# An attention and SoLU kernel: PE planned as two servers, the rows' factor on DVE, more row scaling on POOL

## The chip, the core and the metric

The kernel runs on one core of a Trainium2 chip. The core has five engines, each with its own in-order queue: PE (TensorE, matmuls), ACT (ScalarE), DVE (VectorE), POOL (GpSimd) and SP (SyncE, which here starts every DMA). They wait for each other through semaphores. The metric is the device time of one execution in microseconds (us): the median of three runs is 1230.0 (1227.59 to 1230.04).

## The reference

Four sets of N = 12608 rows of C = 128 numbers go through two attentions with m = 32 inducing points, and every row then through a SoLU layer: 1024 hidden values, a softmax gate, a layer norm and a projection back to 128.

```
def mab(q, kv):
    s = scale * (q @ kv.transpose(0, 2, 1))
    s = s - s.max(-1, keepdims=True)
    a = np.exp(s)
    a /= a.sum(-1, keepdims=True) + 1e-09
    return a @ kv
h = mab(I, x)                       # 32 rows for each set
x = mab(x, h)                       # 4 * 12608 rows
...
h = x @ w_in
e = np.exp(h - np.max(h, axis=-1, keepdims=True))
solu = h * e / (np.sum(e, axis=-1, keepdims=True) + 1e-09)
mu = np.mean(solu, axis=-1, keepdims=True)
var = np.mean((solu - mu) ** 2, axis=-1, keepdims=True)
ln = (solu - mu) / np.sqrt(var + 1e-06) * g_ln
return ln @ w_out
```

## The kernel before

The rows of a set are cut into 99 tiles of 128 rows, 396 tiles in all. Four tiles make a group (25 for each set), three groups a finish (9 for each set, 36 in all).

A set first runs through phase 1, `p1` (the attention of the inducing points: transposes L552, scores L660, sums L742), twelve tiles at a time, then `p2` (the rows' attention weights: scores L857, transposes L552). For the first set, phase 1 fills the first 50 us or so; for the others it is slipped in among the tiles of the set before. Then each tile goes through these steps:

- PE, L959: the tile's h (128 x 1024), in four quarters. The factor of w_in and the attention's result is held as 32 rows in each of PE's four groups of 32 rows; even tiles use the groups 0 and 1 ("pair 0"), odd ones the groups 2 and 3 ("pair 1").
- DVE, L997: negated and normalised h into an `hn` buffer, with its smallest value. These buffers lie partly in a tensor that the profile calls `spare`.
- ACT, L1007: the exponential, with its sum, into an `eu` buffer (or `spare`).
- POOL, L1011: h times the exponential, in place.
- ACT, L1022: the square, for its sum alone. DVE, L1035: a transpose of 32 x 32 blocks into `vt`.
- After four tiles, PE, L1081: the products with w_out, 32 steps of K = 32 for each of the four row groups; a column of ones (129 columns) gives the row sums. The groups 0 and 1 add up in `op_661`, 2 and 3 in `op_662`; each has a single buffer, in which three groups lie side by side.
- After twelve tiles, `evacuate` (L1106) copies `op` to `spare`, on DVE or on ACT, and `finish` turns the sums into one factor for each row: two ACT squares (L1133, L1134), three POOL instructions (L1137 to L1139: the variance), ACT's logarithm and exponential (L1144, L1145: the inverse root), four POOL instructions (L1150 to L1153: a Newton step). All of them are 12 columns wide, one for each quarter of a tile. Then each group's rows are scaled, by four ACT instructions (L1168) or by one of POOL (L1164), and stored.

The order on every engine is written out when the program is built. A planner (`Planner.run`) holds a clock for each engine, costs in ns for each item (`Op`), and priorities (lower goes first). It repeatedly takes the engine that can start soonest, and from the items ready there within `SLACK` the one of the best priority. Where an item has an `alt`, two engines compete for it. PE is one such engine: a "beat" of 225 ns is one step of both pairs, and `beats` puts the products of the other pair beside a tile's quarters (`mm1`) or transposes (`turned_rows`); `driver` emits the products that are left, for both pairs at once. What `beats` pairs is decided once, when the item starts.

Of the kernel before, what the change touches and what calls it, by code (L numbers as in the profile page):

```python
# [13 lines left out]
AF = mybir.ActivationFunctionType  # L14
# [62 lines left out]
WOUT = -11.5
WIN = -18.5
# [47 lines left out]
class Planner:  # L126


    def __init__(self, slack):
# [56 lines left out]

    def _pe(self, start, cost):

        at = start
        while True:  # L190
# [8 lines left out]
            self.busy[k] = self.busy.get(k, 0.0) + took  # L199
            at += took  # L200
            cost -= took / rate
# [3 lines left out]
    def _fill(self, until):  # L205

        for lock in self.scratch:
            if lock.free:
                buf, after = lock.free[0]
                at = max([self.clock["PE"]] + [d.end + AFTER[d.eng]["PE"] for d in after if d is not None])  # L210
# [4 lines left out]
                if at > begun:  # L215
                    self.clock["PE"] = at
# [3 lines left out]
    def run(self):  # L220
        clock = self.clock
        while self.ops:
            first = min(self.ops, key=lambda o: (max(clock[o[0].eng], o[1]), o[3]))
            eng = first[0].eng
            limit = max(clock[eng], first[1]) + self.slack[eng]
            pick = min(
                (o for o in self.ops if o[0].eng == eng and o[1] <= limit),
# [4 lines left out]
            start = max(clock[eng], ready)  # L232
            if eng == "PE" and start - clock[eng] > FILL:
# [3 lines left out]
            end = start + (self._pe(start, op.cost) if eng == "PE" else op.cost)  # L237
            clock[eng] = end
# [1049 lines left out]
```

## Time and profile before

| | |
|---|---|
| median of three runs | 1230.0 us |
| the profiled execution's own time | 1227.1 us |
| its span, first to last instruction | 1225.3 us |
| mean granted TensorE clock | 0.981 |
| DMA, mean rate over the span | 93 GB/s |

A row of the stretches has the stretch in us, its length, then for each engine its busy time and, in brackets, the number of instructions; then the granted clock, and the DMA engines' share and rate. A row of the groups has the line, engine, operation, the tile written and those read, shapes and count; then busy time in us and the mean of one in ns; then how long the engine was idle just before, and on whom it waited. The busy time counts overlapping instructions once. A row of the timeline has its start, its length, and what ran, with the number of merged instructions.

### The profile page before, as it was taken

To read this page: it belongs to the slowest core of one execution; us is meant where nothing else is said; L and a number is where in the kernel's file an instruction comes from. 1 tells how busy PE (TensorE), PEld (TensorE's weight loads), DVE (VectorE), ACT (ScalarE), POOL (GpSimd) and SP (SyncE) were. 2 spreads that over 40 slices of the span, in tenths; PEclk is the share of its full clock that TensorE was granted. 3 is DMA by queue.
4 is the path that set the end of the run, shared out by engine and by line. 5 is a ranking of instruction groups with operands and counts; after the bars stand their busy time and mean duration, and the time that the engine had idled before them with its cause. 6 is when DMAs were issued, how large, how long until landed. Compare 5 with 4: busy or idle time off the path is not lost.

```text
span 1225.3 us, 79047 instructions
## 1 busy us (share of the span) xinstructions
PE 1180.9 (96%) x35679; PEld 1091.4 (89%) x35679; DVE 1114.9 (91%) x1745; ACT 1151.3 (94%) x2479; POOL 1051.5 (86%) x758
## 2 busy tenths in 40 slices
PE   8889999999999999999999999999999999999996
PEld 6678988999899988998999999999888999998986
DVE  5669999999989999999999999999999999999992
ACT  5459999999999999999999999999999999999995
POOL 2568988889888989889889989988898999999994
PEclk9869999999999999999999999999999999999989
DMA  9462443321222324333223144433222121211111
GB/s 362 160 163 74 116 133 116 116 88 35 82 82 87 108 86 131 89 109 102 71 82 100 45 124 128 123 111 90 64 56 82 36 58 55 56 48 45 32 30 35
DMA packets 134866, 113.69 MB, mean 93 GB/s; under 512 B 79072, under 2 KB 87168, under 8 KB 134400
## 3 DMA queue, kind: packets, MB, share of 16 engines
q1 hardware_dynamic: 134528, 108.63, 29.8%
q8 instruction: 279, 4.57, 1.5%
q14 instruction: 59, 0.48, 0.1%
HBM read 54.30 MB, written 52.18 MB: 87 GB/s over the span
## 4 chain that ended last, share of the span: by engine, by line
PE 56%; ACT 21%; DVE 8%; issue 7%; POOL 4%; DMA 2%; SPq 1%; POOLq 0%; ACTq 0%; DVEq 0%
PE op L1081 36%; PE h L959 11%; ACT sq L1022 9%; ACT eu L1007 5%; DVE spare L997 3%; ACT os L1168 2%; POOL eu L1011 2%; DVE vt L1035 2%; PE h L552 2%; ACT spare L1007 1%; PE h L742 1%; PE h L660 1%; PE h L857 1%; DVE spare L1106 1%; DVE hn L997 1%
## 5 line engine op out<-in xcount | busy, mean ns | idle before, releaser
L1081 PE MATMUL op<-wc,vt 32*128 32x129 f32 x25600 | 1000.4, 275 | 11.4 <-ACT spare L1106 4.3
L1081 PEld LDWEIGHTS op<-wc,vt 32*128 32x128 f32 x25600 | 958.2, 186 | 49.3 <-issue 33.0
L1011 POOL TENSOR_TENSOR eu<-spare,eu 128x1024 f32<-128x1024 f32 x192 | 453.3, 2374 | 44.1 <-ACT eu L1007 40.7
L959 PE MATMUL h<-hs,aT 32*128 32x128 f32 x6336 | 438.0, 279 | 10.7 <-DVE spare L997 5.7
L959 PEld LDWEIGHTS h<-hs,aT 32*128 32x128 f32 x6336 | 393.7, 191 | 31.2 <-DVE spare L997 9.6
L1035 DVE STREAM_TRANSPOSE vt<-eu 128x1024 f32<-128x1024 f32 x330 | 401.1, 1228 | 7.2 <-POOL eu L1011 7.1
L1011 POOL TENSOR_TENSOR eu<-hn,eu 128x1024 f32<-128x1024 f32 x138 | 326.3, 2377 | 35.0 <-ACT eu L1007 32.2
L1022 ACT ACTIVATE sq<-eu 128x1024 bf16<-128x1024 f32 x330 | 345.9, 1048 | 6.4 <-POOL eu L1011 3.8
L997 DVE TENSOR_SCALAR_CACHE_REDUCE spare<-h,rn 128x1024 f32<-128x1024 f32 x228 | 286.3, 1263 | 23.5 <-PE h L959 12.6
L997 DVE TENSOR_SCALAR_CACHE_REDUCE hn<-h,rn 128x1024 f32<-128x1024 f32 x168 | 211.3, 1263 | 15.9 <-PE h L959 5.8
L1007 ACT ACTIVATE eu<-spare,nm 128x1024 f32<-128x1024 f32 x192 | 218.8, 1140 | 3.7 <-DVE spare L997 3.6
L1007 ACT ACTIVATE eu<-hn,nm 128x1024 f32<-128x1024 f32 x138 | 157.2, 1139 | 0.0
L1168 ACT ACTIVATE os<-spare,fin 128x128 f32<-128x128 f32 x356 | 110.5, 389 | 2.2 <-POOL fin L1153 1.2
L1011 POOL TENSOR_TENSOR spare<-spare 128x1024 f32<-128x1024 f32 x36 | 85.5, 2374 | 4.1 <-ACT spare L1007 4.1
L1035 DVE STREAM_TRANSPOSE vt<-spare 128x1024 f32<-128x1024 f32 x66 | 81.2, 1231 | 0.0
L1011 POOL TENSOR_TENSOR spare<-hn,spare 128x1024 f32<-128x1024 f32 x30 | 71.2, 2374 | 11.0 <-ACT spare L1007 8.1
L1022 ACT ACTIVATE sq<-spare 128x1024 bf16<-128x1024 f32 x66 | 69.2, 1049 | 2.5 <-POOL spare L1011 1.6
L1022 ACT ACTIVATION_READ_ACCUMULATOR sq<-eu 128x1 f32 x330 | 62.9, 190 | 0.0
L1106 DVE COPY spare<-op 128x774 f32<-128x774 f32 (+1 forms) x40 | 34.6, 865 | 15.1 <-PE op L1081 9.5
L552 PE MATMUL h<-ident,xn 32*128 32x32 f32 x1188 | 46.0, 220 | 0.9 <-issue 0.6
L552 PEld LDWEIGHTS h<-ident,xn 32*128 32x128 f32 x1188 | 44.6, 137 | 2.1 <-issue 1.0
L1007 ACT ACTIVATE spare<-spare,nm 128x1024 f32<-128x1024 f32 x36 | 41.1, 1141 | 0.0
(164 smaller groups left out, 967.8 us busy)
## 6 DMA issues: line engine op xcount, KB each, us to landing
xT<-xd SPq DMA_DIRECT2D x96, 256.0 KB, 3.2
out_dram<-os SPq DMA_DIRECT2D x96, 256.0 KB, 2.5
xn<-in_x_dram SPq DMA_DIRECT2D x73, 256.0 KB, 3.1
xd<-xT SPq DMA_DIRECT2D x72, 256.0 KB, 2.6
dl<-dd SPq DMA_DIRECT2D x396, 1.0 KB, 2.7
xd<-vt SPq DMA_DIRECT2D x7, 768.0 KB, 10.1
spare<-in_x_dram SPq DMA_DIRECT2D x5, 768.0 KB, 12.5
wc<-hn SPq DMA_DIRECT2D x16, 128.0 KB, 3.0
```

Source lines behind the costliest of these rows:

```text
L552: nc.tensor.transpose(out=tr[:h, at : at + M], in_=block[rows, :h], identity=ident[rows, rows])
L660: nc.tensor.matmul(sc[g * M : (g + 1) * M, : nn * M], lhsT=indT, rhs=xT[:, :nn, g * M : (g + 1) * M], start=True, stop=True)
L742: nc.tensor.matmul(pooled[q * M : (q + 1) * M, :], lhsT=ew[:, s, :], rhs=xn[:, s, :], start=(s < 4), stop=(s + 4 >= n))
L959: nc.tensor.matmul(hp[:, cols], lhsT=aT[rows, i // 2, :], rhs=hs[rows, cols], start=True, stop=True)
L997: lambda: nc.vector.tensor_scalar(out=hn, in0=hp, scalar1=rn, scalar2=None, op0=ALU.mult, op1=ALU.min, accum_out=nm),
L1007: "ACT", 1133, lambda: nc.scalar.activation(e, hn, AF.Exp, bias=nm, scale=-1.0, accum_out=G["qe"][:, s, 1:2]), d, rel, srel,
L1011: d = yield Op("POOL", 2330, lambda: nc.gpsimd.tensor_tensor(out=e, in0=hn, in1=e, op=ALU.mult), de, prio=t + PR_MU)
L1022: "ACT", 1040, lambda: nc.scalar.activation(sq, e, AF.Square, scale=1.0 / 32.0, accum_out=G["qe"][:, s, 0:1]), d,
L1035: lambda: nc.vector.transpose(out=G["vtb"][:, : n * FF].rearrange("p (j s t) -> p j s t", j=M, s=n)[:, :, s, :], in_=e.rearrange("p (a f) ...
L1081: nc.tensor.matmul(op[:rows, a - 2 * w, i * (C + 1) : (i + 1) * (C + 1)], lhsT=vt[q, k, :], rhs=wc[q, k, :], start=(k == 0), stop=(k == JB ...
L1106: return lambda: eng(F["raw"][:rows, : 4 * k, :].rearrange("p (j a) c -> p j a c", a=4)[:, :, 2 * w : 2 * w + 2].rearrange("p j a c -> p a ...
L1168: nc.scalar.activation(os[:rows, q, :], raw[:, q, :], AF.Copy, scale=y[:, i0 + q : i0 + q + 1])
```

## The change

**PE as two servers.** The planner gets a clock for each pair, `PE0` and `PE1`; an item of "PE" needs both. Each quarter of a tile's h is now an item of its own pair, so are each three transposes, and each pair has its own `driver`; `beats` and `closing` are gone. **The factor.** ACT's square L1134 goes; three DVE instructions make the variance and three the Newton step, in place of the seven of POOL. **Scaling and evacuation** get priorities by engine, and POOL's cost goes from 1000 to 1040. Most of the tuning numbers change, among them `HN_MORE` (one of the shared buffers goes from `hn` to `eu`) and `FIRST` (the first attention group has six tiles, not four).

```
-JC = 1
-BEAT = 225
-EAGER = 120
+BEAT = 224
-HN_MORE = 4
+HN_MORE = 3
-FIRST = 4
+FIRST = 6
+PR_SA = 13.21
+PR_SP = 41.78
+PR_ED = 17.72
+PR_EA = -19.55
+TURN_NS = 62
+SMALL = 125
+PARTS = {"PE": ("PE0", "PE1")}
-SLACK = {"PE": 0, "ACT": 100, "DVE": 300, "POOL": 0, "SP": 0}
+SLACK = {"PE": 28, "ACT": 52, "DVE": 252, "POOL": 154, "SP": 0}
...
+    def free(self, eng):
+        return max(self.clock[e] for e in PARTS.get(eng, (eng,)))
...
-            first = min(self.ops, key=lambda o: (max(clock[o[0].eng], o[1]), o[3]))
+            first = min(self.ops, key=lambda o: (max(self.free(o[0].eng), o[1]), o[3]))
...
+            same = {eng, "PE"} if eng in PARTS["PE"] else {eng, *PARTS.get(eng, ())}
             pick = min(
-                (o for o in self.ops if o[0].eng == eng and o[1] <= limit),
+                (o for o in self.ops if o[0].eng in same and o[1] <= limit),
...
-            clock[eng] = end
+            for e in PARTS.get(eng, (eng,)):
+                clock[e] = end
...
-        count = -(-len(blocks) // TURNS)
-        return Op("PE", count * BEAT, lambda: beats(count, (1 - w,), some), *after, prio=prio)
+        d = after
+        for i in range(0, len(blocks), TURNS):
+            d = yield Op(f"PE{w}", TURN_NS * min(TURNS, len(blocks) - i) + 10, some(i), d, prio=prio)
+        return d
...
-            d = yield Op("PE", 4 * BEAT, mm1, aT_d, hw_d, rel, prio=t - 50)
-            closing(d)
+            d = yield Op(f"PE{i % 2}", BEAT, quarter(0), aT_d, hw_d, rel, prio=t - 50)
+            for c in range(1, 4):
+                d = yield Op(f"PE{i % 2}", BEAT, quarter(c), d, prio=t - 60)
...
             def step():
-                op.cost = BEAT * beats(JC)
+                p["emit"](2 * w, p["j"])
+                p["emit"](2 * w + 1, p["j"])
+                p["j"] += 1
+
+            d = yield Op(f"PE{w}", BEAT, step, Done("PE", p["ready"]), prio=p["prio"])
...
-            "DVE", 90 + 269 * k, copied(nc.vector.tensor_copy), dop, rel, prio=prio,
-            alt=Op("ACT", 90 + 215 * k, copied(nc.scalar.copy), dop, rel, prio=prio),
+            "DVE", 90 + 269 * k, copied(nc.vector.tensor_copy), dop, rel, prio=prio + PR_ED,
+            alt=Op("ACT", 90 + 215 * k, copied(nc.scalar.copy), dop, rel, prio=prio + PR_EA),
...
-        d = yield Op("ACT", 110, lambda: nc.scalar.activation(part, F["raw"][:rows, :w, C], AF.Square, scale=1.0 / FF), F["out"])
         def variance():
-            gt(out=v, in0=Q, in1=part, op=ALU.subtract)
-            gs(out=v, in0=v, scalar1=0.0, scalar2=None, op0=ALU.max)
-            gt(out=v, in0=v, in1=ep, op=ALU.add)
-        d = yield Op("POOL", 760, variance, fd, d)
+            sums = F["raw"][:rows, :w, C]
+            stt(out=part, in0=sums, scalar=-1.0 / FF**2, in1=sums, op0=ALU.mult, op1=ALU.mult)
+            tt(out=v, in0=part, in1=Q, op=ALU.add)
+            stt(out=v, in0=v, scalar=0.0, in1=ep, op0=ALU.max, op1=ALU.add)
+        d = yield Op("DVE", 3 * SMALL, variance, fd, F["out"])
...
         def newton():
-            gt(out=z, in0=root, in1=root, op=ALU.mult)
-            gt(out=z, in0=z, in1=v, op=ALU.mult)
-            gs(out=z, in0=z, scalar1=-0.5, scalar2=1.5, op0=ALU.mult, op1=ALU.add)
-            gt(out=y, in0=z, in1=root, op=ALU.mult)
-        dy = yield Op("POOL", 1010, newton, d)
+            tt(out=z, in0=root, in1=root, op=ALU.mult)
+            stt(out=z, in0=z, scalar=-0.5, in1=v, op0=ALU.mult, op1=ALU.mult)
+            stt(out=y, in0=z, scalar=1.5, in1=root, op0=ALU.add, op1=ALU.mult)
+        dy = yield Op("DVE", 3 * SMALL, newton, d)
...
-            done = yield Op("ACT", 1170, scaled_act, dy, rel, alt=Op("POOL", 1000, scaled, dy, rel))
+            done = yield Op("ACT", 1170, scaled_act, dy, rel, prio=prio + PR_SA, alt=Op("POOL", 1040, scaled, dy, rel, prio=prio + PR_SP))
```

In the program that comes out, row scalings stand on ACT for 41 groups in place of 89 (164 instructions in place of 356) and on POOL for 59 in place of 11; evacuations on ACT 70 times in place of 32 and on DVE 2 in place of 40. The lines of the new program are a few lower: L1004 is the former L1011, L951 the former L959, L1074 the former L1081, L990 the former L997, L1028 the former L1035, and `op_633`, `op_634` are the former `op_661`, `op_662`.

**POOL and DVE at the thirteenth finish**, in the second set. POOL's queue before, with multiplies around the factor:

```order
L1137 TENSOR_TENSOR fin_111<-dl_110,fin_111 128x12
L1138 TENSOR_SCALAR fin_111<-fin_111 128x12
L1139 TENSOR_TENSOR fin_111<-fin_111 128x12
L1011 TENSOR_TENSOR spare<-spare 128x1024
L1150 TENSOR_TENSOR fin_111<-fin_111 128x12
L1151 TENSOR_TENSOR fin_111<-fin_111 128x12
L1152 TENSOR_SCALAR fin_111<-fin_111 128x12
L1153 TENSOR_TENSOR fin_111<-fin_111 128x12
```

DVE's queue after, at the same finish (`hn_81` is a tile's L990, `small_123` belongs to phase 1 of the next set):

```order
L1130 SCALAR_TENSOR_TENSOR fin_113<-spare 128x12
L1131 TENSOR_TENSOR fin_113<-fin_113,dl_112 128x12
L1132 SCALAR_TENSOR_TENSOR fin_113<-fin_113 128x12
L990 TENSOR_SCALAR hn_81,nm_117<-h_631,rn_97 128x1024
L688 TENSOR_SCALAR small_123,m_126<-h_632,m_126 128x4
L695 TENSOR_SCALAR small_123<-m_126 128x1
L1143 TENSOR_TENSOR fin_113<-fin_113 128x12
L1144 SCALAR_TENSOR_TENSOR fin_113<-fin_113 128x12
L1145 SCALAR_TENSOR_TENSOR fin_113<-fin_113 128x12
L1028 STREAM_TRANSPOSE vt<-spare 128x32x32
```

The seven have left POOL's queue; DVE has two threes instead, with one tile's L990 and two small instructions between them, and transposes behind.

**ACT and POOL where rows are scaled.** ACT's queue before, after the same finish:

```order
L1144 ACTIVATE fin_111<-fin_111 128x12
L1145 ACTIVATE fin_111<-fin_111 128x12
L1007 ACTIVATE eu,qe_108<-spare,nm_115 128x1024
L609 COPY xT<-h_660 128x12x64
L1168 ACTIVATE os_100<-spare,fin_111 128x128 x4
L1168 ACTIVATE os_101<-spare,fin_111 128x128 x4
L1022 ACTIVATE sq,qe_108<-eu 128x1024
```

POOL's queue after, in the second set (L1156 is the former L1164):

```order
L1004 TENSOR_TENSOR spare<-spare 128x1024
L1156 TENSOR_TENSOR os_101<-spare,fin_113 128x512
L1004 TENSOR_TENSOR spare<-spare 128x1024
L1156 TENSOR_TENSOR os_100<-spare,fin_113 128x512
L1004 TENSOR_TENSOR eu<-hn_81,eu 128x1024
```

Where ACT had eight scalings in a row ahead of a tile's square, POOL now has one instruction for each group, between two multiplies.

**PE where the first products start.** Before (`h_659` and `h_660` are tiles' h, each row of `x2` one step of a pair):

```order
L959 MATMUL h_659<-hs_119,aT_96 128x128 x8
L1081 MATMUL op_661<-wc,vt 128x129 x2
L1081 MATMUL op_662<-wc,vt 128x129 x2
L1081 MATMUL op_661<-wc,vt 128x129 x2
L1081 MATMUL op_662<-wc,vt 128x129 x2
```

After:

```order
L951 MATMUL h_631<-hs_119,aT_96 128x128 x8
L951 MATMUL h_632<-hs_119,aT_96 128x128 x4
L1074 MATMUL op_633<-wc,vt 128x129 x2
L951 MATMUL h_632<-hs_119,aT_96 128x128 x2
L1074 MATMUL op_633<-wc,vt 128x129 x4
L951 MATMUL h_632<-hs_119,aT_96 128x128 x2
L1074 MATMUL op_633<-wc,vt 128x129 x2
L1074 MATMUL op_634<-wc,vt 128x129 x2
```

Before, a tile's four quarters were one item, and the products began after it; now products of the other pair stand between the quarters of a tile that is already under way.

More of the change, by code (lines that the diff above doesn't have):

```diff
@@ L88, with kind @@
 DMA_GAP = 25
-BEGIN = {"PE": 1290.0, "ACT": 1700.0, "DVE": 2100.0, "POOL": 1300.0, "SP": 550.0}
+BEGIN = {"PE0": 1290.0, "PE1": 1290.0, "ACT": 1700.0, "DVE": 2100.0, "POOL": 1300.0, "SP": 550.0}
 DMA_RATE = 360.0
 WINDOW = 4096 / 1.2
+def kind(eng):
+    return "PE" if eng[:2] == "PE" else eng
 class Done:
@@ L198, in _pe @@
             took = min(room, cost * rate)
[L199 removed]
+            self.busy[k] = self.busy.get(k, 0.0) + max(0.0, at + took - max(at, self.until))
             at += took
+            self.until = max(self.until, at)
             cost -= took / rate
@@ L209, in _fill @@
                 buf, after = lock.free[0]
-                at = max([self.clock["PE"]] + [d.end + AFTER[d.eng]["PE"] for d in after if d is not None])
+                at = max([self.free("PE")] + [d.end + AFTER[kind(d.eng)]["PE"] for d in after if d is not None])
                 begun = at
@@ L231, in run @@
             op, ready, task = pick[:3]
-            start = max(clock[eng], ready)
-            if eng == "PE" and start - clock[eng] > FILL:
+            eng = op.eng
+            start = max(self.free(eng), ready)
+            if kind(eng) == "PE" and start - self.free("PE") > FILL:
                 self._fill(start - SPARE)
@@ L236, in run @@
             op.fn()
-            end = start + (self._pe(start, op.cost) if eng == "PE" else op.cost)
-            clock[eng] = end
+            end = start + (self._pe(start, op.cost) if kind(eng) == "PE" else op.cost)
+            for e in PARTS.get(eng, (eng,)):
+                clock[e] = end
             if eng == "SP":
@@ L1090, in close @@
             give(TURN[w], None)
-        ready = max(d.end + AFTER[d.eng]["PE"] for a in (G["turned"], rel, wc_ready.after) for d in a if d is not None)
+        ready = max(d.end + AFTER[kind(d.eng)]["PE"] for a in (G["turned"], rel, wc_ready.after) for d in a if d is not None)
         stream[w].update(j=0, emit=emit, ready=ready, close=close, prio=t + PR_G2)
-        idle = flow["idle"]
+        idle = flow[w]["idle"]
         if idle.waiting:
@@ L1259, in set_attention_then_solu_kernel @@
     spawn(main(), 0)
-    spawn(driver(), 0)
+    for w in range(2):
+        spawn(driver(w), 0)
     plan.run()
```

119 lines of the change are left out of this document (48 added, 71 removed).

## The prediction

> **What bounds the kernel now.** I read the page first, then the busy time by stretches (0 to 80 us, where the first batch is read; 80 to 1200 us, where all four engines work on tiles; the end).
>
> ```profile
> span 1225.3 us, 79047 instructions
> ...
> PE 1180.9 (96%) x35679; PEld 1091.4 (89%) x35679; DVE 1114.9 (91%) x1745; ACT 1151.3 (94%) x2479; POOL 1051.5 (86%) x758
> ...
> PE 56%; ACT 21%; DVE 8%; issue 7%; POOL 4%; DMA 2%; SPq 1%; POOLq 0%; ACTq 0%; DVEq 0%
> ```
>
> ```profile
> core 0: us, PE busy (x) PEld busy (x) DVE busy (x) ACT busy (x) POOL busy (x), PEclk, DMA share, GB/s
> 0.00:80.00 80.00, 66.36 (x703) 51.09 (x705) 48.80 (x135) 42.53 (x97) 32.13 (x34) 0.87 0.67 229
> 80.00:1200.00 1120.00, 1098.77 (x34490) 1025.22 (x34492) 1060.56 (x1604) 1098.52 (x2358) 1009.69 (x707) 0.99 0.29 84
> 1200.00:1225.30 25.30, 15.79 (x504) 15.07 (x496) 5.53 (x6) 10.28 (x27) 9.66 (x19) 0.89 0.15 41
> ```
>
> The chain of work that ended last lies 56% on PE, and PE is busy for 98% of the middle. But ACT is busy for 98.1% too (1098.5 of 1120), DVE for 94.7%, POOL for 90.2%. Of the two full ones, PE is full only by name, as the timeline and two groups show:
>
> ```profile
> 601.28 0.28 PE L1081 MATMUL op<-wc,vt 32*128 32x129 f32 x2
> 601.29 0.28 PE L959 MATMUL h<-hs,aT 32*128 32x128 f32 x2
> 601.39 0.28 PE L1081 MATMUL op<-wc,vt 32*128 32x129 f32 x2
> ...
> L1081 PE MATMUL op<-wc,vt 32*128 32x129 f32 x25600 | 1000.4, 275 | 11.4 <-ACT spare L1106 4.3
> L959 PE MATMUL h<-hs,aT 32*128 32x128 f32 x6336 | 438.0, 279 | 10.7 <-DVE spare L997 5.7
> ```
>
> A matmul here occupies one group of 32 rows, and four of them start within 0.11 us: two of one pair of row groups (L1081), two of the other (L959). The 25600 + 6336 of them would, four at a time, take 31936 / 4 x 0.11 = 878 us. So the row groups have about a fifth of the middle spare, which is lost where one pair's matmul stands alone. ACT has nothing of the kind: what it does, it does one after the other. **ACT is the bound of the middle**, with PE tied to it through tiles that wait for each other and DVE 38 us of work behind.
>
> **The change, engine by engine.** ACT first:
>
> ```profile
> L1168 ACT ACTIVATE os<-spare,fin 128x128 f32<-128x128 f32 x356 | 110.5, 389 | 2.2 <-POOL fin L1153 1.2
> ...
> L1106 ACT COPY spare<-op 128x774 f32<-128x774 f32 (+1 forms) x32 | 25.2, 788 | 4.2 <-DVE spare L1106 2.5 <-PE op L1081 1.3 <-DVE small L694 0.2
> L1134 ACT ACTIVATE fin<-spare 128x12 f32<-128x12 f32 (+1 forms) x36 | 7.7, 213 | 3.6 <-DVE spare L1106 3.5
> ```
>
> Row scalings on ACT fall from 356 to 164 instructions by the order. They overlap at their ends (356 x 389 ns would be 138 us, the union is 110.5), so one is worth 110.5 / 356 = 0.31 us, and 192 of them 59.6 us. The 36 squares of L1134 go: 7.7 us. The evacuations of the products come over from DVE, 70 in place of 32: 38 x 0.79 = 30 us. ACT: -59.6 - 7.7 + 30 = **-37 us**, nearly all in the middle: 1098.5 becomes 1061.
>
> POOL, by its instructions on the tile of factors and the scalings among them:
>
> ```profile
> 0.00:1225.30 1225.30, 65.53 (x263) 0.98 0.32 93
> ...
> L1164 POOL TENSOR_TENSOR os<-spare,fin 128x512 f32<-128x512 f32 (+1 forms) x11 | 11.5, 1042 | 0.6 <-POOL fin L1153 0.2
> L1138 POOL TENSOR_SCALAR fin<-fin 128x12 f32<-128x12 f32 (+1 forms) x36 | 8.6, 239 | 3.2
> L1137 POOL TENSOR_TENSOR fin<-dl,fin 128x12 f32<-128x12 f32 (+1 forms) x36 | 7.8, 217 | 11.2 <-ACT fin L1134 11.1
> ```
>
> 252 small instructions leave: 65.5 - 11.5 = 54 us, and with them the 0.09 us of idle ahead of each chained one (3.2 / 36) and waits such as the 11.2 us for ACT. 48 scalings come: 48 x 1.04 = 50 us. POOL: **-4 us** busy and some 25 us less waiting; it stays at 90%.
>
> DVE:
>
> ```profile
> L1106 DVE COPY spare<-op 128x774 f32<-128x774 f32 (+1 forms) x40 | 34.6, 865 | 15.1 <-PE op L1081 9.5
> L349 DVE MEMSET tiny<- 128x1 f32 x1 | 0.1, 59 | 0.0
> L758 DVE SCALAR_TENSOR_TENSOR acc<-acc,small,h 128x128 f32<-128x128 f32 x24 | 8.0, 335 | 2.9 <-PE h L742 2.7
> L720 DVE TENSOR_SCALAR l<-l,small 128x1 f32<-128x1 f32 x26 | 6.7, 258 | 2.2 <-ACT eT L711 1.5 <-ACT os L711 0.3
> L883 DVE RECIPROCAL rn<-nr 128x12 f32<-128x12 f32 (+3 forms) x37 | 7.5, 204 | 1.5 <-ACT nr L882 1.4
> ...
> 42.04 0.16 DVE L786 TENSOR_SCALAR small<-bank_e 128x1 f32<-128x1 f32 x1
> 42.23 0.16 DVE L787 RECIPROCAL small<-small 128x1 f32<-128x1 f32 x1
> ```
>
> 38 copies go: 38 x 0.865 = 33 us. 36 x 6 = 216 small instructions come. None of their form beside a working POOL stands in this trace; the nearest rows bound them at 0.06 us (L349) and 0.34 us (L758, ten times as wide), 13 to 72 us in all. A reciprocal of the same 12 columns takes 0.20, and two small instructions of which one needs the other start 0.19 us apart (L786, L787). I take 0.19: 41 us. DVE: -33 + 41 = **+8 us**; with the ends, -20 to +39. In the middle 1060.6 becomes 1069: DVE, not ACT, is now the fullest by a hair.
>
> The waits. Before, DVE idled 59 us of the middle, much of it because PE or ACT was late:
>
> ```profile
> L997 DVE TENSOR_SCALAR_CACHE_REDUCE spare<-h,rn 128x1024 f32<-128x1024 f32 x228 | 286.3, 1263 | 23.5 <-PE h L959 12.6 <-ACT eu L1007 6.1 <-issue 1.7
> L997 DVE TENSOR_SCALAR_CACHE_REDUCE hn<-h,rn 128x1024 f32<-128x1024 f32 x168 | 211.3, 1263 | 15.9 <-PE h L959 5.8 <-ACT eu L1007 5.6 <-ACT spare L1007 1.0
> ```
>
> 39 us stand before L997 alone. The change adds one: the second three of the six wait on DVE for ACT's logarithm and exponential (0.21 and 0.20 us, L1144 and L1145 in the rows of the end, below); behind them in DVE's queue stand transposes, for which PE waits, and further L997, for which ACT does. The order puts an L997 of 1.26 us and some small ones between the threes, which covers the two; without that cover it is 36 x 0.4 = 15 us, and with one of ACT's exponentials ahead of them (1.14 us, the next row) 36 x 1.55 = 56.
>
> ```profile
> L1007 ACT ACTIVATE eu<-spare,nm 128x1024 f32<-128x1024 f32 x192 | 218.8, 1140 | 3.7 <-DVE spare L997 3.6
> ```
>
> One buffer goes from the hn ring to the eu ring; I cost it at nothing, as L997 waits little for POOL in these rows.
>
> PE issues the same matmuls; only their neighbours change. After, each quarter of a tile's h and each three transposes is an item of its own pair, so the other pair's products stand where its own clock puts them. Where one item stood with a partner and now doesn't, 0.22 us (two steps of 0.11) are lost, and the other way round won. I see both in the order and cost it at 0, with -10 to +10.
>
> The end. After the last evacuation, nothing else runs beside the factor:
>
> ```profile
> 1216.34 0.21 ACT L1134 ACTIVATE fin<-spare 96x4 f32<-96x4 f32 x1 [2.95 <-DVE spare L1106]
> 1216.63 0.20 POOL L1137 TENSOR_TENSOR fin<-dl,fin 96x4 f32<-96x4 f32 x1 [3.54 <-ACT fin L1134]
> ...
> 1217.45 0.21 ACT L1144 ACTIVATE fin<-fin 96x4 f32<-96x4 f32 x1 [0.90 <-POOL fin L1139]
> 1217.69 0.20 ACT L1145 ACTIVATE fin<-fin 96x4 f32<-96x4 f32 x1
> ...
> 1218.82 0.20 POOL L1153 TENSOR_TENSOR fin<-fin 96x4 f32<-96x4 f32 x1
> ```
>
> L1134 goes (0.3 us), seven POOL steps of 0.29 become six of 0.19 (0.9 us), and the last scaling moves from POOL (1.04) to ACT (4 x 0.31): -1 us. At the start the first attention group has six tiles in place of four; I leave it at 0, with -3 to +3.
>
> **The sum.** The middle is the fullest engine's work and the idle time that it keeps. ACT kept 21 us as the fullest. DVE kept 59 beside an ACT that was late; ACT now has 59 to spare itself (1120 - 1061), and I let DVE keep half of its own, 30, the new wait for ACT's two activations among it: 1069 + 30 = 1099, 21 us less than 1120. With the end, 1227.1 (the profiled execution's own time, 1225.3 and 1.8 around it) - 21 - 1 = 1205. The median of the runs, 1230.0, is 2.9 above the profiled one; half of that on top gives **1206**. With ACT's 21 us for DVE's idle time, it is 1090 and 1197; with small instructions at 0.06 us, ACT is the fullest again, 1061 + 21 = 1082 and 1189; at 0.34, DVE's 1100 + 30 = 1130 gives 1237.
>
> **The rivals.** *DVE takes ACT's place.* DVE keeps all of its 59 us: 1128, 8 us more than now, and 1235. For it: the two engines were close, and their waits on PE are not touched by name. Against it: ACT's lateness is what ran through those waits. It decides where DVE's idle time stays above 51 us. If the change does nothing for the time, since the new order pairs PE no better and ACT's work merely turns into idle time, it is 1225 to 1230, a case between.
>
> *The small instructions wait for POOL.* This one ends slower:
>
> ```profile
> 886.46 4.69 POOL L1011 TENSOR_TENSOR eu<-spare,eu 128x1024 f32<-128x1024 f32 x2 [0.97 <-ACT eu L1007]
> 886.90 2.00 DVE L789 TENSOR_SCALAR accn<-acc,small 128x128 f32<-128x128 f32 x1
> ...
> L789 DVE TENSOR_SCALAR accn<-acc,small x4: 286/286/1996, 43.8 to 886.9; 128x128 f32<-128x128 f32 x4
> L720 DVE TENSOR_SCALAR l<-l,small x26: 231/268/275, 17.0 to 882.0; 128x1 f32<-128x1 f32 x26
> L883 DVE RECIPROCAL rn<-nr x37: 166/202/229, 51.5 to 1152.3; 128x12 f32<-128x12 f32 x27, 128x8 f32<-128x8 f32 x5, 128x7 f32<-128x7 f32 x4, 128x4 f32<-128x4 f32 x1
> ```
>
> The last three rows give the shortest, median and longest in ns. L789 takes 0.29 us at its median, and 2.00 the time that it starts inside a POOL multiply; it ends at 888.90, just after that multiply (half of 4.69 from 886.46: 888.8). Some DVE instructions thus stand still until POOL's ends. If the six are of that kind, the first of each three finds POOL at work 9 times in 10 (its share of the middle) and waits half of 2.35 us: 72 x 0.9 x 1.17 = 76 us on DVE. Its 1069 become 1145, with the 30 us of idle time 1175: 55 more than 1120, and 1282; 1252 where DVE idles for nothing else. If the second and third wait for whole multiplies, it is 1350 and more. It decides from 21 / 216 = 0.1 us of wait for each. Against it: narrow DVE instructions never stood still, though POOL is at work 9 times in 10. L720 reads three operands from SBUF, of one element each, and takes 0.28 us at most in all 26; L883, as wide as the six but with one input, 0.23 at most. All six have two inputs in SBUF. [...]
>
> **How the numbers follow.** Forecast, 1188 to 1227: 0.72. DVE as before, or nothing: 0.13, of which 0.08 within 0.2% of 1230.0 (2.5 us, about what a measurement of this kernel can tell from no change) and 0.05 above. Waits for POOL: 0.15. So faster 0.72, same 0.08, slower 0.20. The range runs from 1188 to 1245: it takes in the first two cases with the dear small instructions, and leaves out the waits for POOL (0.15) and a few hundredths below.
>
> **What would show it.** ACT's busy time near 1114 in all (1151.3 - 37), DVE's near 1123, POOL's near 1047. The six on DVE at about 0.2 us each; if their means lie near 1 us, the rival of POOL is right, and they will end where POOL's multiplies end. If DVE's idle time before the line that scales h keeps its 39 us, DVE took ACT's place. The forecast is wrong, too, if PE's spare fifth is smaller than I think: then ACT and DVE both idle more, and PE's waits on evacuations, now behind ACT's activations alone, grow.

## The result, and the profile after

The changed kernel takes 1381.1 us (median of 4 runs, 1379.1 to 1383.6), the kernel before 1229.2 us beside it: ratio **1.1234** (95% interval 1.1193 to 1.1275). It is 152 us slower, where 24 us less were forecast (1206 against 1230.0). The page of the kernel after: its span, the busy time of the engines and the head of the chain of work that ended last.

```profile
span 1381.8 us, 78852 instructions
...
PE 1239.5 (90%) x35688; PEld 1152.3 (83%) x35688; DVE 1256.8 (91%) x1922; ACT 1128.1 (82%) x2289; POOL 1049.0 (76%) x555
...
PE 48%; DVE 29%; ACT 11%; issue 8%; DMA 2%; POOL 1%; SPq 1%; DVEq 0%; ACTq 0%; POOLq 0%
```

ACT lost 23 us of work and POOL 2.5, where 37 and 4 were forecast. But DVE is 142 us busier, not 8, and its share of the chain went from 8% to 29%. The groups by line tell where, DVE alone (busy us, mean ns of one, then the idle time before):

```profile
L1131 DVE TENSOR_TENSOR fin<-fin,dl 128x12 f32<-128x12 f32 (+1 forms) x36 | 64.2, 1784 | 1.8 <-DVE fin L1130 0.7
L1130 DVE SCALAR_TENSOR_TENSOR fin<-spare 128x12 f32<-128x12 f32 (+1 forms) x36 | 51.3, 1426 | 1.0 <-ACT spare L1099 0.9
L1132 DVE SCALAR_TENSOR_TENSOR fin<-fin 128x12 f32<-128x12 f32 (+1 forms) x36 | 28.3, 785 | 3.6
L1143 DVE TENSOR_TENSOR fin<-fin 128x12 f32<-128x12 f32 (+1 forms) x36 | 13.0, 361 | 1.0 <-ACT fin L1138 1.0
L1144 DVE SCALAR_TENSOR_TENSOR fin<-fin 128x12 f32<-128x12 f32 (+1 forms) x36 | 12.4, 344 | 1.2
L1145 DVE SCALAR_TENSOR_TENSOR fin<-fin 128x12 f32<-128x12 f32 (+1 forms) x36 | 8.2, 228 | 1.2
```

The 216 small instructions take 177.4 us in all, 0.82 each, where 0.19 was forecast. A mean hides what they do; the timeline of one finish shows it (start us, length us, engine and line), DVE first, then POOL:

```profile
163.93 0.55 DVE L875 TENSOR_REDUCE nr<-a 128x12 f32<-128x384 f32 x1
164.40 0.34 DVE L752 SCALAR_TENSOR_TENSOR acc<-acc,small,h 128x128 f32<-128x128 f32 x1
164.65 0.84 DVE L1130 SCALAR_TENSOR_TENSOR fin<-spare 128x12 f32<-128x12 f32 x1
165.53 2.30 DVE L1131 TENSOR_TENSOR fin<-fin,dl 128x12 f32<-128x12 f32 x1
167.94 0.17 DVE L1132 SCALAR_TENSOR_TENSOR fin<-fin 128x12 f32<-128x12 f32 x1
...
163.09 4.72 POOL L1004 TENSOR_TENSOR eu<-hn,eu 128x1024 f32<-128x1024 f32 x2 [0.53 <-ACT eu L1000]
169.95 1.04 POOL L1156 TENSOR_TENSOR os<-spare,fin 128x512 f32<-128x512 f32 x1 [2.14 <-issue]
```

POOL's two products end at 165.45 (half of 4.72 after 163.09) and at 167.81. L1130 ends at 165.49 and L1131 at 167.83: each is over just behind one of them. L1132 begins when POOL is idle and takes 0.17. Two others, L875 and L752, lie inside the first product and are not held up: a reduction, and a product of which one input, the tile `h`, lies in PSUM (27 of the 32 of L752 begin inside an instruction of POOL, and none takes more than 0.36 us). Counted over the whole trace, 134 of the 216 begin while POOL is idle, and none of these takes more than 0.18 us; 82 begin inside an instruction of POOL and take 155.5 us together. Each of the 75 above 0.4 us ends 0.02 to 0.04 us after an instruction of POOL ends.

The waits (us in all, times, longest) tell how the standstill goes on:

```profile
POOL eu L1004 <- ACT eu L1000: 114.2, 93, 3.5
ACT fin L1137 <- DVE fin L1132: 85.4, 35, 3.7
```

ACT's logarithm L1137 is next in ACT's fixed order while DVE still stands: 85.4 us in 35 waits. The exponentials behind it come late, and POOL waits for those. This also drains POOL, so that the second three of the six mostly find it idle (98 of 108); they are the cheap ones.

### The profile page after: what moved, and what is told of

Read it like the earlier page. It is cut to its first block, busy times and chain, and to the rows that moved or that the text cites. A ratio compares the mean times of both kernels' runs of the same rounds, so it can differ in the third digit from the quotient of the medians.

```text
span 1381.8 us, 78852 instructions
## 1 busy us (share of the span) xinstructions
PE 1239.5 (90%) x35688; PEld 1152.3 (83%) x35688; DVE 1256.8 (91%) x1922; ACT 1128.1 (82%) x2289; POOL 1049.0 (76%) x555
## 3 DMA queue, kind: packets, MB, share of 16 engines
q1 hardware_dynamic: 134672, 108.63, 26.5%
## 4 chain that ended last, share of the span: by engine, by line
PE 48%; DVE 29%; ACT 11%; issue 8%; DMA 2%; POOL 1%; SPq 1%; DVEq 0%; ACTq 0%; POOLq 0%
PE op L1074 31%; PE h L951 8%; DVE vt L1028 6%; DVE hn L990 5%; ACT sq L1015 5%; DVE fin L1131 5%; DVE spare L990 4%; DVE fin L1130 3%; PE h L543 2%; ACT eu L1000 2%; DVE fin L1132 2%; PE h L851 1%; PE h L736 1%; ACT spare L1000 1%; ACT spare L1099 1%
## 5 line engine op out<-in xcount | busy, mean ns | idle before, releaser
L1074 PE MATMUL op<-wc,vt 32*128 32x129 f32 x25600 | 1058.4, 284 | 16.3 <-DVE vt L1028 11.7
L1074 PEld LDWEIGHTS op<-wc,vt 32*128 32x128 f32 x25600 | 1014.7, 196 | 44.0 <-issue 23.4
L951 PE MATMUL h<-hs,aT 32*128 32x128 f32 x6336 | 461.6, 288 | 24.2 <-DVE hn L990 17.3
L951 PEld LDWEIGHTS h<-hs,aT 32*128 32x128 f32 x6336 | 415.1, 199 | 49.7 <-DVE hn L990 18.8
L1004 POOL TENSOR_TENSOR eu<-spare,eu 128x1024 f32<-128x1024 f32 x141 | 333.7, 2370 | 64.2 <-ACT eu L1000 57.5
L1004 POOL TENSOR_TENSOR eu<-hn,eu 128x1024 f32<-128x1024 f32 x141 | 333.3, 2372 | 59.7 <-ACT eu L1000 56.7
L1028 DVE STREAM_TRANSPOSE vt<-eu 128x1024 f32<-128x1024 f32 x282 | 344.7, 1232 | 3.4 <-POOL eu L1004 3.2
L990 DVE TENSOR_SCALAR_CACHE_REDUCE spare<-h,rn 128x1024 f32<-128x1024 f32 x199 | 251.3, 1264 | 32.4 <-PE h L951 29.6
L990 DVE TENSOR_SCALAR_CACHE_REDUCE hn<-h,rn 128x1024 f32<-128x1024 f32 x197 | 248.3, 1263 | 21.6 <-PE h L951 18.5
L1000 ACT ACTIVATE eu<-spare,nm 128x1024 f32<-128x1024 f32 x141 | 161.4, 1145 | 12.9 <-DVE spare L990 12.8
L1004 POOL TENSOR_TENSOR spare<-spare 128x1024 f32<-128x1024 f32 x58 | 137.5, 2374 | 23.7 <-ACT spare L1000 21.8
L1004 POOL TENSOR_TENSOR spare<-hn,spare 128x1024 f32<-128x1024 f32 x56 | 132.5, 2372 | 28.1 <-ACT spare L1000 26.4
L1028 DVE STREAM_TRANSPOSE vt<-spare 128x1024 f32<-128x1024 f32 x114 | 139.7, 1232 | 0.5 <-POOL spare L1004 0.5
L1156 POOL TENSOR_TENSOR os<-spare,fin 128x512 f32<-128x512 f32 (+1 forms) x59 | 61.5, 1044 | 78.4 <-issue 46.1
L1137 ACT ACTIVATE fin<-fin 128x12 f32<-128x12 f32 (+1 forms) x36 | 7.6, 212 | 85.4 <-DVE fin L1132 85.4
L1099 ACT COPY spare<-op 128x774 f32<-128x774 f32 (+1 forms) x70 | 53.3, 761 | 23.7 <-PE op L1074 16.1
```

The costliest lines, as they stand in the source:

```text
L951: nc.tensor.matmul(hp[:, cols], lhsT=aT[rows, i // 2, :], rhs=hs[rows, cols], start=True, stop=True)
L990: lambda: nc.vector.tensor_scalar(out=hn, in0=hp, scalar1=rn, scalar2=None, op0=ALU.mult, op1=ALU.min, accum_out=nm),
L1000: "ACT", 1133, lambda: nc.scalar.activation(e, hn, AF.Exp, bias=nm, scale=-1.0, accum_out=G["qe"][:, s, 1:2]), d, rel, srel,
L1004: d = yield Op("POOL", 2330, lambda: nc.gpsimd.tensor_tensor(out=e, in0=hn, in1=e, op=ALU.mult), de, prio=t + PR_MU)
L1028: lambda: nc.vector.transpose(out=G["vtb"][:, : n * FF].rearrange("p (j s t) -> p j s t", j=M, s=n)[:, :, s, :], in_=e.rearrange("p (a f) ...
L1074: nc.tensor.matmul(op[:rows, a - 2 * w, i * (C + 1) : (i + 1) * (C + 1)], lhsT=vt[q, k, :], rhs=wc[q, k, :], start=(k == 0), stop=(k == JB ...
```

## Experiments

Theory 1: the six stand still because of something that DVE shares with POOL. Theory 2: the two-server order of PE is at fault. Theory 3: the round trip DVE-ACT-DVE in the fixed orders of DVE and ACT is, or any small DVE instruction beside POOL suffers.

| run | what runs | us | ratio to before (95%) | the six (or fewer), us |
|---|---|---|---|---|
| after | the changed kernel | 1381.1 | 1.1234 (1.1193-1.1275) | 177.4 |
| e1 | after, factor on ACT and POOL | 1239.6 | 1.0103 (1.0066-1.0139) | none |
| e2 | before, with the six | 1354.6 | 1.1047 (1.1005-1.1090) | 131.5 |
| e3 | after, plain one-input forms | 1379.4 | 1.1237 (1.1212-1.1262) | 177.7 |
| e11 | e3 with accumulators | 1213.3 | 0.9870 (0.9829-0.9911) | 33.8 |
| e5 | after, stand-in reductions | 1213.8 | 0.9842 (0.9815-0.9868) | 36.2 |
| e4 | after, POOL's product in halves | 1323.8 | 1.0782 (1.0743-1.0822) | 144.6 |
| e6 | after, planned at 820 ns | 1394.6 | 1.1295 (1.1259-1.1330) | 189.3 |
| e7 | after, only Newton on DVE | 1297.5 | 1.0520 (1.0464-1.0575) | 86.9 (three) |
| e9 | after, six reductions | 1234.7 | 1.0042 (1.0020-1.0065) | 37.8 |
| e10 | before, six reductions | 1259.3 | 1.0249 (1.0216-1.0282) | 38.1 |
| e8 | after, two reductions, no Newton | 1226.4 | 0.9949 (0.9923-0.9974) | 12.5 (two) |
| e12 | after, three reductions, no Newton | 1229.2 | 0.9967 (0.9947-0.9987) | 19.3 (three) |

The last column is the sum of the busy times of the groups of the factor's DVE instructions; for e11, reading the accumulators adds 18.0 us.

**Which part of the change.** Run e1 undoes the factor alone, e2 makes the factor alone.

```
 e1: after, in finish()
-        d = yield Op("DVE", 3 * SMALL, variance, fd, F["out"])
+        d = yield Op("ACT", 110, lambda: nc.scalar.activation(part, F["raw"][:rows, :w, C], AF.Square, scale=1.0 / FF), F["out"])
+        d = yield Op("POOL", 760, variance, fd, d)
...
-        dy = yield Op("DVE", 3 * SMALL, newton, d)
+        dy = yield Op("POOL", 1010, newton, d)
 e2: before, the same lines the other way round, and SMALL = 125
```

> The changed kernel with the rows' factor made as before (the square on ACT, seven small instructions on POOL, none on DVE); the two-server plan, all its numbers and the lean of the scalings stay. If the six DVE instructions stand still behind POOL's multiplies (theory 1), their 177 us leave DVE and the time falls from 1381 to 1195-1225 us, below the kernel before or close to it. If the two-server order of PE or its tuning is at fault (theory 2), it stays above 1330 us. If the round trip DVE-ACT-DVE in DVE's and ACT's fixed order is at fault (theory 3), 1195-1225 as well, since the trip is now POOL-ACT-POOL.

> The kernel before with nothing but the factor on six small DVE instructions, planned at 125 ns each. Theory 1: 216 instructions of which a third stand still, 140-180 us on DVE in place of 41, time 1340-1390 us. Theory 2: 1225-1245 us, since PE's order is that of before. Theory 3: above 1300 us too, but with instructions of about 0.17 us and the idle time of DVE or ACT grown instead.

e1 takes 1239.6 us, e2 1354.6. The factor on DVE costs 141.5 us in the new order and 126.7 in the old one (against 1227.9 for the kernel before, run beside it): theory 2 is not needed for the loss. e2's six, 131.5 us, are a little under the foretold 140. e1 is above the foretold 1225, and 1.0% slower than the kernel before: with the factor on POOL, the rest of the change gains nothing. It is not the factor alone that moves there: given other costs, the planner writes another order, and e1's has the scalings of 66 groups on ACT (264 instructions) and of 34 on POOL, in place of 41 and 59. Theory 3 is still open after these two.

**What in the instructions.** Both runs leave number, width of the result, place and chain of the six alone and change their form; what they compute then is not the factor. In the traces of the kernel after, e3, e5 and e11 below, the instructions of ACT, DVE and POOL stand in the same order, one for one (e11's accumulator reads aside).

```
 e3: after, each of the six as, for instance,
-            tt(out=v, in0=part, in1=Q, op=ALU.add)
+            ts(out=v, in0=part, scalar1=1.0, scalar2=0.0, op0=ALU.mult, op1=ALU.add)
 e5: after, each as a reduction over two neighbours, for instance
+            nc.vector.tensor_reduce(out=t, in_=pairs, op=ALU.add, axis=AX.X)
```

> The changed kernel with each of the six replaced by an instruction of the same width, at the same place and in the same chain, that reads one tensor of SBUF instead of two (part of the sums alone, v of part alone, z and y of root alone: the factor leaves out the mean of squares, the floor and the Newton step). Theory 1: none of the 216 is over 0.4 us, sum 36-45 us instead of 177, time 1195-1225 us. Theory 3 (the chain in the queues) and theory 2: the time stays above 1330 us, for the chain, the queues and PE's order are those of the changed kernel; if length of a small DVE instruction beside a POOL multiply has nothing to do with its second input, their sum stays about 177 us.

> The changed kernel with the six as reductions over pairs (TENSOR_REDUCE, one tensor of SBUF, same number, same 12 columns out, same places, same chain of six; the factor's arithmetic is left out: maxima and sums stand for the products). In the traces so far no reduction of DVE is longer inside a POOL instruction than outside, while e3's plain TENSOR_SCALAR stood still as long as the two-input forms. Theory 1, sharpened (what the form shares with POOL decides, and a plain TENSOR_SCALAR from SBUF shares it too): none of the 216 above 0.4 us, sum 36-50 us, time 1195-1245 us, near the 1240 us of the run with the factor back on POOL. Theory 3 (chain in the queues, or any small DVE instruction beside POOL): sum stays near 177 us and the time above 1330 us.

e3 is a clear miss for theory 1 as I had put it: with one input each, the six take 177.7 us and the kernel 1379.4. So a second input is not needed for it. It isn't the chain either: e5 has the same chain and takes 1213.8 us. In e5's groups (five of the six stand under one helper's line), none stands still, though 198 of the 216 begin inside an instruction of POOL:

```profile
PE 1172.5 (97%) x35688; PEld 1087.2 (90%) x35688; DVE 1112.7 (92%) x1922; ACT 1117.2 (92%) x2289; POOL 1047.4 (86%) x555
...
L1128 DVE TENSOR_REDUCE fin<-fin 128x12 f32<-128x24 f32 (+1 forms) x180 | 31.0, 172 | 10.9 <-ACT fin L1130 2.2 <-ACT fin L1141 1.8
L1133 DVE TENSOR_REDUCE fin<-spare 128x12 f32<-128x24 f32 (+1 forms) x36 | 5.2, 144 | 1.0 <-ACT spare L1099 0.9
```

This leaves the question what a plain TENSOR_SCALAR with one input has in common with the two-input forms. Run e11 gives each of e3's six an accumulator. Two of them, L1131 and L1143, differ in nothing else; in the other four the second operation or a constant changes too.

```
-            ts(out=v, in0=part, scalar1=1.0, scalar2=0.0, op0=ALU.mult, op1=ALU.add)
+            ts(out=v, in0=part, scalar1=1.0, scalar2=0.0, op0=ALU.mult, op1=ALU.add, accum_out=F["sum"][:rows])
```

> The run with six one-input TENSOR_SCALARs once more, each now with an accumulator written out beside its result (as DVE's big multiply from PSUM has it), which adds a small instruction of about 0.08 us behind each; the factor's arithmetic is left out as there. In the traces the accumulating form never was longer inside a POOL instruction, the plain one of 12 columns was. [...] If any TENSOR_SCALAR of 12 columns from SBUF waits: as without accumulators, 160-180 us and 1370-1400 us.

It takes 1213.3 us, 166 less than e3, and its six take 33.8 us: not the 1370 to 1400 and the 160 to 180 of a wait in any TENSOR_SCALAR of 12 columns from SBUF. The rows of line L1131 by its instructions, in the kernel after, in e3 and in e11 (shortest, median and longest in ns; then the first and last start):

```profile
L1131 DVE TENSOR_TENSOR fin<-fin,dl x36: 159/2254/2301, 126.7 to 1374.7; 128x12 f32<-128x12 f32 x32, 96x4 f32<-96x4 f32 x4
```

```profile
L1131 DVE TENSOR_SCALAR fin<-fin x36: 166/2265/2300, 125.9 to 1372.9; 128x12 f32<-128x12 f32 x32, 96x4 f32<-96x4 f32 x4
```

```profile
L1131 DVE TENSOR_SCALAR_CACHE_REDUCE fin<-fin x36: 152/166/168, 124.5 to 1200.0; 128x12 f32<-128x12 f32 x32, 96x4 f32<-96x4 f32 x4
```

Same line, same 12 columns, same neighbours: 2.25 us in the median, 2.27, and 0.17. The same finish as above shows it in e11's timeline, under two products of POOL again:

```profile
163.57 0.17 DVE L1130 TENSOR_SCALAR_CACHE_REDUCE fin<-spare 128x12 f32<-128x12 f32 x1
163.67 0.08 DVE L1130 DVE_READ_ACCUMULATOR fin<-spare 128x1 f32 x1
163.78 0.17 DVE L1131 TENSOR_SCALAR_CACHE_REDUCE fin<-fin 128x12 f32<-128x12 f32 x1
...
162.00 4.73 POOL L1004 TENSOR_TENSOR eu<-hn,eu 128x1024 f32<-128x1024 f32 x2 [0.54 <-ACT eu L1000]
```

So the **form** decides, as theory 1 in its sharpened wording has it: of these instructions at the same place, two inputs in SBUF (2254 ns in the median) and a plain TENSOR_SCALAR from SBUF to SBUF (2265) stand under POOL's products, while an accumulating TENSOR_SCALAR (166) and a reduction (172 in the mean, e5) run. What the forms that stand share with POOL, no run shows.

**How long, and where it could be put.** Run e4 halves what they wait for, e6 tells the planner the price, e7 moves only the Newton step.

```
 e4: -   nc.gpsimd.tensor_tensor(out=e, in0=hn, in1=e, op=ALU.mult)
     +   for c in (slice(0, 512), slice(512, 1024)):
     +       nc.gpsimd.tensor_tensor(out=e[:, c], in0=hn[:, c], in1=e[:, c], op=ALU.mult)
 e6: -SMALL = 125
     +SMALL = 820
 e7: e1, and in it the Newton step as in the changed kernel:
     -   dy = yield Op("POOL", 1010, newton, d)
     +   dy = yield Op("DVE", 3 * SMALL, newton, d)
```

> The changed kernel with POOL's product (128x1024, 2.37 us, 311 times) in two halves of 512 columns, some 1.2 us each, the factor left on DVE. Theory 1: a standing instruction waits for the half that runs and no longer for the whole: the long ones end behind a half, their mean falls from 1.9 to about 1.0 us, the sum of the six from 177 to 90-120 us, time 1290-1340 us if POOL itself loses nothing by the halves. Theories 2 and 3: within 15 us of 1381, or slower by what 311 more POOL instructions cost (0.05 us each, 16 us).

> The changed kernel, the planner told 820 ns for each of the six (their measured mean) in place of 125. If the loss comes from a plan that counts on too small a price, and a true price would mend it: below 1300 us. If the instructions stand still wherever they are put, since POOL is busy three quarters of the time: 1340-1395 us, with the sum of the six still above 140 us.

> The changed kernel with only the Newton step on DVE; the variance is back on ACT and POOL. In the changed kernel the three of the variance took 144 us of the 177, the three of the Newton step 34, since 30 of 36 of the latter began while POOL stood idle, waiting for just this. If each instruction pays only for the POOL instruction inside which it starts: the three take 20-45 us and the time is 1235-1270 us. If the cost is per instruction whatever it meets: half of the 142 us between the changed kernel and the run with the factor back, near 1310 us.

In e4's groups the product's halves take 1.28 us each and overlap a little (353.6 us for 141 pairs), so a pair takes 0.14 more than the whole (the expectation's 0.05 was a guess), but the time falls by 57 us:

```profile
L1006 POOL TENSOR_TENSOR eu<-spare,eu 128x512 f32<-128x512 f32 x282 | 353.6, 1278 | 49.9 <-ACT eu L1000 29.6 <-issue 16.0 <-ACT nr L876 1.9
...
L1134 DVE SCALAR_TENSOR_TENSOR fin<-spare 128x12 f32<-128x12 f32 (+1 forms) x36 | 43.4, 1207 | 1.0 <-ACT spare L1103 0.9
L1135 DVE TENSOR_TENSOR fin<-fin,dl 128x12 f32<-128x12 f32 (+1 forms) x36 | 35.0, 972 | 2.2 <-DVE fin L1134 1.1
L1136 DVE SCALAR_TENSOR_TENSOR fin<-fin 128x12 f32<-128x12 f32 (+1 forms) x36 | 32.0, 888 | 3.6
```

The second, L1135, fell from 1784 ns to 972, as theory 1 wants. The sum, 144.6 us, missed the foretold 90 to 120, for two reasons. More of the six begin inside an instruction of POOL, 124 in place of 82, at 1.04 us each in place of 1.90; the third of the three now meets a half of its own (888 ns against 785). And four of the 36 L1134 stand through five or six halves in a row, 5.2 to 6.6 us, 23.5 us together: that the wait is over with the instruction that runs holds for most, not for all. (POOL makes 396 products, not the 311 of the expectation.) In e6 the six still take 189 us and the time is no better, as the second alternative had it; the planner, told the price, only takes scalings from POOL (39 of L1156 in place of 59) and gives them to ACT. e7 is another miss: the three of the Newton step took 33.6 us in the kernel after and take 86.9 alone:

```profile
L1144 DVE TENSOR_TENSOR fin<-fin 128x12 f32<-128x12 f32 (+1 forms) x36 | 33.3, 926 | 8.4 <-ACT fin L1139 8.2
L1145 DVE SCALAR_TENSOR_TENSOR fin<-fin 128x12 f32<-128x12 f32 (+1 forms) x36 | 28.7, 797 | 3.8
L1146 DVE SCALAR_TENSOR_TENSOR fin<-fin 128x12 f32<-128x12 f32 (+1 forms) x36 | 24.9, 693 | 1.2
```

I read it so: they had been cheap because the variance, standing ahead of them, had drained POOL (10 of the 108 began inside one of its instructions). With POOL kept at work, 57 of the 108 do, among them 29 of the 36 L1144. Such a price can't be carried from one order to another.

**A version that is faster than the changed kernel.** Reductions can compute the factor: with the column of ones in `wc` set to 1/1024, a negated product of the mean with itself, a sum and a maximum make the variance, and two products and a sum the Newton step.

```
 e9: after (e10: before), SMALL = 175, in finish(); red is nc.vector.tensor_reduce over the innermost axis
+            red(S, often(F["raw"][:rows, :w, C], 2), ALU.mult, True)
+            red(T, four[:, :, 0:3], ALU.add)
+            red(v, four[:, :, 2:4], ALU.max)
...
+            red(R3, often(root, 3), ALU.mult)
+            red(N2, last[:, :, 0:2], ALU.mult, True)
+            red(y, last[:, :, 2:4], ALU.add)
 e12: e9 without the last three and ACT's two copies for them; e8: square and sign on ACT, two reductions
```

> The changed kernel with the whole factor, Newton step included, from six reductions of DVE over 24 or 36 columns (products, sums and maxima of one interleaved tensor); ACT makes two small copies more for each finish (0.19 us, 36 times each, 14 us). Theory 1: the six take 38-45 us and never stand still, DVE about as busy as with the six stand-in reductions (1113 us), ACT about 1130 us; time 1205-1235 us, 0.98-1.005 of the kernel before. If it was the left-out arithmetic or the shorter chain that saved time there, and not the form: above 1300 us.

> The kernel before with the same six reductions in its finish, and its own plan (no two servers, its own numbers, no lean of the scalings). It tells what the rest of the change is worth once nothing stands still. If the two-server plan and the lean are worth what the prediction gave to ACT (37 us less on the bound): this is at 1225-1245 us, 15-30 us behind the run on the changed kernel. If they are worth nothing: level with it within 5 us, both some 10-20 us below the kernel before, as the small instructions leave POOL.

> A version of the changed kernel that computes the factor and leaves out the Newton step alone (the factor is as exact as ACT's logarithm and exponential): ACT makes the square, its negative and the floor, DVE adds and takes the maximum in two reductions, POOL makes nothing of it. Theory 1: two reductions at about 0.15-0.25 us, 72 of them some 15 us, no wait; DVE 25 us less and ACT about 8 us more than with six reductions, POOL 60 us less than before; time 1190-1235 us, level with the kernel before or below it. Theories 2 and 3: above 1300 us.

> The run with six reductions without its Newton step (the factor is as exact as ACT's logarithm and exponential): three reductions on DVE, and ACT's three small instructions of the changed kernel, without the two copies and without the round trip behind them. DVE some 20 us and ACT some 14 us less than in that run (1234.7 us). If ACT, DVE and the wait of the finish set the time: 1205-1225 us, below the kernel before. If PE, busy 97% of the stand-in runs, sets it by now: 1222-1236 us.

e9 computes the whole factor and is 146 us faster than the changed kernel; its six take 37.8 us. It ends 0.4% above the kernel before. e8 (0.9949) and e12 (0.9967) are below both kernels, by half a per cent and a third, but they leave out the Newton step, which the kernel before computes; what that kernel would gain without it was not run. e12 came out at 1229.2, not at the 1205 to 1225 that ACT, DVE and the finish as the bounds had meant, and PE is busy for 96% of it. e10 tells what the rest of the change is worth beside the same six reductions: the order of before takes 1259.3 and that of after 1234.7, so **24.6 us** for the two servers, the shift of scalings to POOL and the new numbers together. That is no worth of its own: with the factor on POOL the new order is 11.7 us slower than the old one (e1), and with the six that stand 26.5 us slower (the kernel after against e2). And e10 lies above the foretold 1245: in the old order the reductions cost 30 us against the factor on POOL, though they take 0.18 us each.

## Why the prediction was wrong, point by point

- **The six small instructions: the step that failed.** "I take 0.19: 41 us" is measured as 0.82 and 177.4 us. The rows behind the 0.19 were narrow instructions of other forms: a reciprocal, and TENSOR_SCALARs of one column. The prediction said that none of their form beside a working POOL stood in the trace, and then priced them by width.
- **The rival of POOL: right in mechanism, given 0.15.** I held against it that "narrow DVE instructions never stood still". That is true of those rows and says nothing of the six: those rows are of one column or of another form, and at 12 columns the form decides (e3 against e11). A row of the trace of before, L758, has two full inputs and did not wait (0.35 us at most), though 21 of its 32 begin inside an instruction of POOL; one input is in PSUM, which I passed over. L789, the one that I saw waiting, is a plain TENSOR_SCALAR, as e3's. The rival's price was right where it let the second and third wait for whole products ("1350 and more"), too low with one wait for each three (1252, 1282). In part that was luck: of the second three, only 10 of 108 begin inside an instruction of POOL. Its sign came as announced: means near 1 us, ends where POOL's products end.
- **The counts and the other engines: right.** With forms that don't stand, e5 has ACT at 1117.2 us (1114 forecast), DVE at 1112.7 (1123), POOL at 1047.4 (1047). Its small instructions cost 0.17 us. So scalings, squares, copies and the evacuations moved to ACT were sized well.
- **DVE's idle time: not halved, even where nothing stands.** e5 takes 1213.8 us where 1206 was forecast, but partly by luck. The sum let DVE keep 30 of its 59 us of idle time in the middle, beside 1069 us of work. e5's middle, cut at the same distance from both ends, has 1051.3 us of work and 56.8 of idle time:

```profile
80.00:1188.10 1108.10, 1085.60 (x34396) 1014.51 (x34396) 1051.29 (x1763) 1058.73 (x2152) 1002.54 (x515) 1.00 0.30 84
```

Two errors, 27 us too little and 18 too much, nearly cancel. By the prediction's own sign, idle time above 51 us, this is the rival in which DVE takes ACT's place. But ACT, relieved, idles for 49.4 us there as well, and PE is busy for 98% as before, which points at PE as what holds both; no run shows it. And e9, which computes the whole factor, takes 1234.7 us.
- **The new wait for ACT: small by itself.** 15 to 56 us were named for a lost cover. In e5, with the same chain, DVE waits 1.8 us in all for ACT's exponential (L1141 in the row of L1128); in the kernel after, it is ACT that waits for DVE (85.4 us at L1137), as a result of the standstill.
- **From 141 us of standing to 168 us of time.** Against e5, the six take 141.2 us more, DVE 144.1 us more, and the span grew by 168.4: DVE's idle time went from 100.7 us to 125.0. Most of that is DVE's wait for PE before L990, 48.1 us in place of 28.1; the kernel after first, then e5:

```profile
L990 DVE TENSOR_SCALAR_CACHE_REDUCE spare<-h,rn 128x1024 f32<-128x1024 f32 x199 | 251.3, 1264 | 32.4 <-PE h L951 29.6
L990 DVE TENSOR_SCALAR_CACHE_REDUCE hn<-h,rn 128x1024 f32<-128x1024 f32 x197 | 248.3, 1263 | 21.6 <-PE h L951 18.5
```

```profile
L990 DVE TENSOR_SCALAR_CACHE_REDUCE hn<-h,rn 128x1024 f32<-128x1024 f32 x197 | 248.0, 1261 | 18.5 <-PE h L951 14.8
L990 DVE TENSOR_SCALAR_CACHE_REDUCE spare<-h,rn 128x1024 f32<-128x1024 f32 x199 | 250.5, 1261 | 15.3 <-PE h L951 13.3
```

PE is late in two ways. It waits for L990 in its turn, and its matmuls take longer, 288 ns in place of 278; again the kernel after, then e5:

```profile
L951 PE MATMUL h<-hs,aT 32*128 32x128 f32 x6336 | 461.6, 288 | 24.2 <-DVE hn L990 17.3 <-DVE spare L990 3.5 <-ACT xT L604 1.4
```

```profile
L951 PE MATMUL h<-hs,aT 32*128 32x128 f32 x6336 | 441.5, 278 | 8.5 <-DVE hn L990 2.4 <-ACT aT L891 2.0 <-DVE spare L990 1.7
```

The longer matmuls go with a lower granted clock behind a finish. Here L1130 and L1131 stand, one behind the other, from 491.8 to 495.6 us (kernel after):

```profile
485.40:491.80 6.40, 6.40 (x198) 5.63 (x198) 6.37 (x10) 6.37 (x11) 3.38 (x3) 1.00 0.49 146
491.80:498.20 6.40, 3.12 (x100) 2.82 (x96) 6.16 (x15) 3.48 (x12) 3.87 (x3) 1.00 0.69 188
498.20:501.60 3.40, 3.40 (x72) 3.40 (x69) 2.70 (x4) 2.73 (x7) 2.59 (x2) 0.51 0.38 107
```

PE is busy for 3.1 of 6.4 us, and then has half of its clock for 3.4 us. From 90 us to 15 us before the end, such stretches add up to 163.8 us in the kernel after and 170.7 in e3, to 13.7 in the kernel before, 3.4 in e5 and none in e11. In the kernel after, PE starts 16.9 matmuls a us in them and 28.5 outside. Of DVE's idle time 21.9 us lie in them, in e5 3.4: that is 18.5 of the 24 us. So in these five kernels most of the half clock goes with the standstill; how much of the time it costs was only read from the traces, since none of them has the standstill without it.

What stays open: why the change without its six (e1) is 1.0% slower than the kernel before (its order keeps ACT busy for 1145.4 us, 28 more than e5's), why the reductions cost 30 us in the old order, and why e9 takes 21 us more than e5 with DVE 8 us and ACT 9 us busier.

## What to carry to other kernels

Before moving small work from one engine to another, ask of its form, before its size, whether it runs beside a busy neighbour, and look in the trace for a row of the same form, with its operands in the same memories, that starts inside that neighbour's long instructions. Here reductions (0.17 us in the mean, e5), accumulating forms (0.17 in the median, e11) and a product with one input from PSUM (0.36 at most, L752) ran beside POOL, and those are the forms to give DVE there; where the two-input forms stayed, POOL's product in halves made them wait less on the whole (145 us in place of 177), though some stood through five or six halves in a row (e4). DVE's standstill also drained the others (ACT waited for it for 85.4 us, POOL for ACT's exponentials for 114.2), and its price didn't carry over from one order to the next: 141 us of it cost 168 in the kernel after (against e5), the 87 us of e7's three cost 58 (against e1).

## What the runs showed of the hardware

- A plain TENSOR_SCALAR of 128x12 from SBUF to SBUF stood still under POOL's product (2265 ns in the median, e3); with an accumulator it took 166 ns and 83 more for reading that out (e11). The instruction with more to do was the cheaper one beside POOL. Four columns didn't protect: the three 96x4 instructions of e3's L1131 that begin inside an instruction of POOL took 2.26 to 2.27 us.
- A plain TENSOR_SCALAR of one column didn't stand: in the kernel after, 24 of the 36 of L695 begin inside an instruction of POOL, and none takes longer than 156 ns. What spares it, no run shows.

```profile
L695 DVE TENSOR_SCALAR small<-m x36: 153/154/156, 13.3 to 1011.3; 128x1 f32<-128x1 f32 x36
```

- In the kernel after, each of the 75 waits ended 0.02 to 0.04 us behind an instruction of POOL. Of the 27 L1130 above 0.4 us, 26 saw one such end, and 28 of the 36 L1131, next in DVE's queue, began inside an instruction of POOL and took 2.10 to 2.30 us. Not all went so: one L1130 stood for two products (4.30 us), and in e4 four of L1134 stood through five or six halves (5.2 to 6.6 us). What decides it, no run shows.
- From 491.8 to 498.2 us of the kernel after PE was busy for 3.12 of 6.40 us, and in the 3.4 us behind that the granted clock was 0.51; half of the clock is there in 32 stretches of that kernel's middle and in one of e5's.
